# The order of the first transfers in a retention and two-layer-pair kernel

## The chip, the cores and the metric

One core of one Trainium2 chip runs the whole program. The metric is device time in microseconds (us); the figure of a kernel is the median of its runs. The kernel before took 1101.65 us (three runs, 1098.88 to 1103.2). The engines are named as the profile names them: PE multiplies matrices (PEld loads its weights), DVE works elementwise, ACT evaluates functions and copies, POOL is the general engine, SP issues nearly all transfers. Every engine takes its instructions in the order in which they are written.

## The reference, cut to what matters

```python
# q, k, v: (4, 8, 768, 64) = batch, heads, tokens, head size
gamma = 1.0 - 2.0 ** (-5.0 - np.arange(H))
for t in range(S):                                   # retention
    state = gamma * state + np.einsum('bhd,bhe->bhde', k[:, :, t], v[:, :, t])
    y[:, :, t] = scale * np.einsum('bhd,bhde->bhe', q[:, :, t], state)
x = y.transpose(0, 2, 1, 3).reshape(B * S, H * D)    # 3072 x 512
h = x @ w_in;  x = (h - np.tanh(h)) @ w_out          # 512 -> 2048 -> 512
h = x @ w_in2                                        # 512 -> 2048
x = np.where(h > 0, h, np.exp(np.minimum(h, 0)) - 1) @ w_out2
```

All weights and inputs are float32 (the weights arrive as 64-bit words, which the kernel converts).

## The kernel before

**The work.** The retention is cut into 24 steps: six chunks of 128 tokens, each for four batch entries. Step s needs three inputs: queries and keys with heads on the partitions (one transfer, `qk`, 512 KB), values (`v`, 256 KB) and keys with tokens on the partitions (`kn`, 256 KB). On PE a step is a group of score products (`sc`), an output (`oe`, `oo`) made of the state times the queries and of the values times the masked scores (`pt`), and a state update, which multiplies `v` and `kn`. DVE masks the scores (L297), scales the queries in place (L339) and scales `kn` in place (L343). Four steps fill one block of 512 tokens, and block b is then multiplied: product n of the first layer gives `h` from the block `x` and weight tile (0, f), ACT and DVE turn `h` into the gate `g` (h - tanh h by a polynomial where h is small), and the second layer adds weight tile (1, f) times `g` into four accumulators `acc`. Every factor is split in a high and a low part, and three of the four partial products are summed (`three`, L389 to L395; all large products of PE have line L392). So one product is 12 matmuls of 128x512. The two later layers (names `x`, `w`, `z`, `xo`, `wo`, `zo`) use a scheme with seven products for eight.

**The weights at the start.** A raw weight tile (512 KB, `raw`) is fetched (L305), converted by one pass of ACT (L308) and two of DVE (L312, L316) to `w32`, then split by ACT (L288) and DVE (L291). `jobs0` lists the tiles in the order in which they are wanted: (0, 0), (0, 1), (0, 2), (1, 0), (0, 3), (1, 1), and so on. For the first two blocks the products run over f = 0 to 7 first, block 0 and then block 1, so products 0 to 7 need sixteen tiles converted, and block 0 needs steps 0 to 3 and block 1 steps 4 to 7.

**The opening, in written order (L398 to L535).** Warm-up products, the transfers of steps 0 to 3, tiles 0 and 1, the queries of step 4 (`qk[B]`), tiles 2 and 3; then the work of steps 0 to 3 with the conversion of tiles 0 and 1 between; then, in buffers that earlier work has used (`va`, `ka`), the values and keys of step 4, tiles 4 to 11, and at the end the queries and keys of step 5 (`qa`, `kb`). Each transfer also waits until the eighth transfer before it has landed.

**The planner (class Plan, L57 to L243).** Everything behind the opening is given to it as operations with readers, writers, lengths and buffers. It walks through time with one list of ready operations for each engine, gives buffers from pools (`A_TAGS`, `B_TAGS` and so on; those that the opening holds stand in `taken`, and `had` hands them over) and takes on each engine the ready operation that is due first. PE's order is fixed. What it writes down is the order of the instructions; on the chip the semaphores decide the times. `ret_load` (L651) requests the inputs of a step, `loads` (L849) names the product after which it may, and converted weights of the second layer pair are stored to memory in pieces (`w2d`, `w3d`) and loaded again later, as are those of the first pair (`w1d`).

Of the kernel before, what the change touches and what calls it, by code (L numbers as in the profile page):

```python
# [8 lines left out]
F32 = mybir.dt.float32  # L9
# [9 lines left out]
P = 128  # L19
TB = 512  # L20
# [36 lines left out]
class Plan:  # L57
# [10 lines left out]
    def op(self, eng, dur, fn, r=(), w=(), lat=0.1, rel=0, due=None, name=""):  # L68
        o = Op()
        o.eng, o.fn, o.dur, o.lat, o.rel, o.name, o.due = eng, fn, dur, lat, rel, name, due  # L70
        o.n, o.deps, o.users, o.bufs = len(self.ops), set(), [], []

        def split(x):
            return x if isinstance(x, tuple) else (x, None)

        def met(table, key):
            return [v for k, v in table.items() if key is None or k is None or k == key]

        for x in r:
            b, k = split(x)  # L80
            o.deps.update(met(b.w, k))
        for x in w:
            b, k = split(x)
            o.deps.update(met(b.w, k))
            for ops in met(b.rd, k):
                o.deps.update(ops)
        for x in r:
            b, k = split(x)
            b.rd.setdefault(k, []).append(o.n)
            if b not in o.bufs:  # L90
                o.bufs.append(b)
        for x in w:
            b, k = split(x)
            for key in [i for i in b.w if k is None or i == k]:
                del b.w[key]
            for key in [i for i in b.rd if k is None or i == k]:
                del b.rd[key]
            b.w[k] = o.n
            if b not in o.bufs:
                o.bufs.append(b)  # L100
        for b in o.bufs:
            if b.group and not b.held and not b.left:
                c, k = self.groups.get(b.group, (b.cls, 0))
                self.groups[b.group] = c, k + 1
            b.left += 1
        o.deps.discard(o.n)
        self.ops.append(o)
        o.pe = None
        if eng == "PE":
            o.pe = len(self.pe)  # L110
            self.pe.append(o)
        return o

    def run(self):
# [4 lines left out]
        t, start = 0.0, {}  # L119
# [12 lines left out]
            else:  # L132
                o.late = min([o.late] + [e - o.dur - o.lat for e in ends])
        left = {o.n: len(o.deps) for o in ops}
        ready = {e: [] for e in ("ACT", "DVE", "SP", "POOL")}
        busy = dict.fromkeys(("PE", "ACT", "DVE", "SP", "POOL"), 0.0)
        state = {"dma": 0.0, "pe": 0, "at": 0.0}
        events = [(0.0, -1)]
        order = []

# [25 lines left out]
        def begin(o, t):  # L166
            for b in o.bufs:
                if b.cls != "D" and not b.held:
                    b.slot = self.free[b.cls].pop(0)
                    b.held = True  # L170
                    if b.group:
                        self.used[b.group] += 1
                        c, k = self.groups[b.group]
                        self.groups[b.group] = c, k - 1
            end = t + o.dur + o.lat
            if o.eng in ("SP", "POOL"):
                busy[o.eng] = t + (0.08 if o.eng == "SP" else 1.0)
                state["dma"] = max(state["dma"], t) + o.dur
                end = max(state["dma"], t) + 2.2
            else:  # L180
                busy[o.eng] = t + o.dur
            heapq.heappush(events, (busy[o.eng], -1))
            heapq.heappush(events, (end, o.n))
            order.append((o, t))
# [5 lines left out]
        while events:  # L190
# [18 lines left out]
            while moved:  # L209
                moved = False  # L210
                if busy["PE"] <= now and state["pe"] < len(self.pe):
                    o = self.pe[state["pe"]]
# [34 lines left out]
def retention_moe_kernel(ctx: ExitStack, tc: tile.TileContext, dims, ins, out):  # L247
    nc = tc.nc
    B, H, S, D, DM, DFF = dims
# [6 lines left out]
    NF = DFF // P  # L256
# [27 lines left out]
    def place(cls, tag, shape, dtype, name):  # L284
        return (ps if cls == "P" else sb).tile(shape, dtype, tag=tag, name=name)
# [18 lines left out]
    def fetch_(raw, job):  # L304
        nc.sync.dma_start(out=raw, in_=ins[f"w{job[0]}"][job[1]])  # L305
# [72 lines left out]
    def load_qk(t, s):  # L378
        nc.sync.dma_start(out=t, in_=ins["qkv"][s][:, 0:2, :])

    def load_v(t, s):
        nc.sync.dma_start(out=t, in_=ins["qkv"][s][:, 2, :])

    def load_kn(t, s):
        nc.sync.dma_start(out=t, in_=ins["qkv"][s][:, 3, :])
# [11 lines left out]
    with tc.manual_schedule():  # L397
# [23 lines left out]
        def fetch(i):  # L421
            job = jobs0[i]
            raw[job] = place("A", f"a{i}", [P, TB], I64, f"raw{job[0]}_{job[1]}")
            fetch_(raw[job], job)
# [11 lines left out]
        def convert_c(i):  # L436
            job = jobs0[i]
            t = wt[job] = place("A", f"a{i}", [P, 2, TB], F32R, f"w{job[0]}_{job[1]}")
            copy(t[:, 0, :], w32[job])
            return lambda: sub(t[:, 1, :], w32[job], t[:, 0, :].bitcast(F32))  # L440

        qk = {s: stage[:, s] for s in range(B)}
        v, kn, pt, sc, o0 = {}, {}, {}, {}, {}
# [8 lines left out]
            kn[s] = kn23[:, s - 2, :] if s > 1 else place("B", "k" + "ab"[s], [P, TB], F32, f"kn{s}")  # L452
            load_kn(kn[s], s)
        fetch(1)
        qk[B] = place("A", "qb", [P, 2, TB], F32, f"qk{B}")
        load_qk(qk[B], B)
        fetch(2)
        fetch(3)
        x0 = place("X", "x0", [P, 2, KC, TB], F32R, "x0")

        def scores0(s):
# [45 lines left out]
        for j in range(2):  # L507
            ds.append(place("P", f"b{6 + j}", [P, 2, NP, D], F32, f"dsp{j}"))
            for c in range(2):
                s = 2 * j + c  # L510
# [4 lines left out]
            st[j] = place("B", f"t{j}", [P, 2, NP, D], F32, f"st{j}")  # L515
            nc.vector.tensor_copy(out=st[j], in_=ds[j])
        lo1 = convert_c(1)
        v[B] = place("B", "va", [P, TB], F32, f"v{B}")
        load_v(v[B], B)
        kn[B] = place("B", "ka", [P, TB], F32, f"kn{B}")  # L520
        load_kn(kn[B], B)
        for i in range(4, 12):
            fetch(i)
        scores0(B)
        convert_b(2)
        lo1()
# [2 lines left out]
        scale_k_(kn[B])  # L529
        convert_a(3)  # L530
        convert_b(3)
        qk[B + 1] = place("A", "qa", [P, 2, TB], F32, f"qk{B + 1}")
        load_qk(qk[B + 1], B + 1)
        kn[B + 1] = place("B", "kb", [P, TB], F32, f"kn{B + 1}")
        load_kn(kn[B + 1], B + 1)  # L535

        taken = {"x0", "qa", "qb", "pt", "va", "ka", "kb", "t0", "t1", "s2", "s3"} | {f"a{i}" for i in range(12)}
        slots = {"A": A_TAGS, "B": B_TAGS, "C": C_TAGS, "X": X_TAGS, "P": P_TAGS}  # L540
        plan = Plan(
            {c: [t for t in tags if t not in taken] for c, tags in slots.items()},
# [4 lines left out]
        )  # L547
        op = plan.op

        def had(cls, slot, ap):  # L550
            return Buf(cls, name=slot, ap=ap, slot=slot)

        dr = {id(t): Buf("D", name="d") for t in (*x1d, *w1d, *w2d, w3d)}

# [4 lines left out]
        X[0] = had("X", "x0", x0)  # L559
        for i in range(2):  # L560
            W[jobs0[i]] = had("A", f"a{i}", wt[jobs0[i]])
        for i in range(2, 12):
            RAW[jobs0[i]] = had("A", f"a{i}", raw[jobs0[i]])
        for i in range(2, 4):
            W32[jobs0[i]] = had("B", f"s{i}", w32[jobs0[i]])
        QK = {B: had("A", "qb", qk[B]), B + 1: had("A", "qa", qk[B + 1])}
        V = {B: had("B", "va", v[B])}
        KN = {B: had("B", "ka", kn[B]), B + 1: had("B", "kb", kn[B + 1])}
        PT = {B: had("A", "pt", pt[B])}
        ST = {j: had("B", f"t{j}", st[j]) for j in range(2)}  # L570

# [4 lines left out]
        def dma(fn, size, r=(), w=(), rel=0, due=None, eng="SP", name="dma"):  # L576
            return op(eng, size * DMA, fn, r=r, w=w, rel=rel, due=due, name=name)
# [73 lines left out]
        def ret_load(s, rel):  # L651
            if s not in QK:
                t = QK[s] = Buf("A", [P, 2, TB], F32, f"qk{s}", "qk")
                dma(lambda: load_qk(t.ap, s), 4096, w=[t], rel=rel)
            t2 = V[s] = Buf("B", [P, TB], F32, f"v{s}", "v")
            dma(lambda: load_v(t2.ap, s), 2048, w=[t2], rel=rel)
            if s // B == NCH - 1:
                return
            if s not in KN:
                t3 = KN[s] = Buf("B", [P, TB], F32, f"kn{s}", "kn")  # L660
                dma(lambda: load_kn(t3.ap, s), 2048, w=[t3], rel=rel)
            k = KN[s]
            op("DVE", DVE5, lambda: scale_k_(k.ap), w=[k], name=f"scalek{s}")

        def ret_scores(s):
            q = QK[s]
            c = [Buf("P", [P, NP, P], F32, f"sc{s}_{j}") for j in range(2)]
# [6 lines left out]
        def ret_out(s):  # L674
            b, c = divmod(s, B)
            q, vv, p, sv = QK.pop(s), V.pop(s), PT.pop(s), ST[c // 2]
            even = Buf("P", [P, NP // 2, P], F32, f"oe{s}")
# [4 lines left out]
            if not last:  # L682
                k = KN.pop(s)
                op("PE", 0.6, lambda: state_mm(state_view(odd.ap), vv.ap, k.ap), r=[k, vv], w=[(odd, 1)], lat=0.2, name=f"state{s}")
# [158 lines left out]
        events = {0: [("out", B)]}  # L843
        for s in range(B + 1, NSTEP):
            b, k = s // B - 1, s % B
            at = 2 * k - 1 if b == 0 else FA + NF - 2 + 2 * k if b == 1 else b * NF + 4 * k + 1
            events.setdefault(at, []).append(("scores", s))
            events.setdefault(at + 1, []).append(("out", s))
        loads = {at - 2: s for at, l in events.items() for what, s in l if what == "scores"}  # L849
        for s in [loads.pop(k) for k in sorted(loads) if k < 0]:  # L850
            ret_load(s, 0)

# [284 lines left out]
```

## Time and profile before

| | before |
|---|---|
| median of the runs | 1101.65 us |
| the profiled execution | 1101.44 us, its span 1099.6 us |
| PE busy | 1075.6 us, 98% of the span |
| DVE, ACT, POOL busy | 82%, 65%, 0% |
| memory traffic | 217 GB/s over the span |

The profile is of one execution. Its page gives the busy time of each engine, forty slices of the span and the costliest groups of instructions; the trace behind it answers by stretch, by engine and by who waited for whom. A busy share near 100% says that an engine sets the pace, but not where it stood: that is read from the list of its waits and from the timeline around each. Idle time of an engine is put down to the one that released it. A time that begins a row is counted from the start of the span.

### The profile page before, as it was taken

The numbers are of one execution on the slowest core, as the hardware profiler recorded it, in microseconds if no ns is written. First come the engines' busy times: TensorE is split into PE (matmuls) and PEld (weight loads), VectorE is DVE, ScalarE is ACT, GpSimd is POOL, SyncE is SP. The second block draws the span as 40 slices with busy tenths as digits, with TensorE's granted clock in tenths as the row PEclk, the third lists the DMA queues.
The fourth block names the chain that finished last, engine by engine and source line by source line (L and its number), as shares of the span: only waits on it lengthen the run. The fifth ranks groups of instructions, "written<-read, shape, count | busy, mean of one in ns | idle before, by whom it ended". The sixth has DMA issues, their size and how long they took to land.

```text
span 1099.6 us, 15843 instructions
## 1 busy us (share of the span) xinstructions
PE 1075.6 (98%) x5745; PEld 877.7 (80%) x5745; DVE 905.5 (82%) x1516; ACT 709.6 (65%) x1290; POOL 3.9 (0%) x8
## 2 busy tenths in 40 slices
PE   7699999999999999999999999999999999999998
PEld 5488888888888877788888888888888888888887
DVE  6698899768888888888889769895977987878964
ACT  2557685546556655665678579964588864689652
POOL 0000000000000000000000000000000000000000
PEclk9799999999999999999999999999999999999999
DMA  9733366438666766776688569246966058863253
GB/s 331 272 115 134 154 230 210 116 116 248 231 221 225 254 220 221 273 257 238 248 294 288 192 235 383 110 153 217 388 233 233 15 216 320 330 213 132 112 213 134
DMA packets 99230, 239.86 MB, mean 218 GB/s; under 512 B 7632, under 2 KB 42448, under 8 KB 96464
## 3 DMA queue, kind: packets, MB, share of 16 engines
q1 hardware_dynamic: 98000, 235.96, 59.7%
q0 software_dynamic: 576, 2.10, 1.1%
q8 instruction: 45, 0.74, 0.3%
q10 hardware_dynamic: 576, 0.79, 0.2%
q14 instruction: 33, 0.27, 0.1%
HBM read 186.39 MB, written 52.43 MB: 217 GB/s over the span
## 4 chain that ended last, share of the span: by engine, by line
PE 82%; DMA 7%; DVE 7%; ACT 2%; issue 1%; SPq 1%; DVEq 0%
PE acc L392 19%; PE h L392 17%; PE xo L392 12%; PE x L392 12%; PE z L392 6%; PE zo L392 6%; PE wo L392 3%; PE w L392 3%; DMA kn<-qkv 3%; DMA qk<-qkv 2%; PE sc L332 2%; DMA raw<-w 1%; PE oe L362 1%; DVE pt L297 1%; DVE y L733 1%
## 5 line engine op out<-in xcount | busy, mean ns | idle before, releaser
L392 PE MATMUL acc<-g,w 128*128 128x512 f32 x1152 | 283.6, 395 | 0.1
L392 PE MATMUL h<-x,w 128*128 128x512 f32 x1152 | 278.5, 391 | 0.0
L392 PEld LDWEIGHTS h<-x,w 128*128 128x128 f32 x1152 | 217.0, 189 | 45.5 <-issue 0.2
L392 PEld LDWEIGHTS acc<-g,w 128*128 128x128 f32 x1152 | 214.1, 189 | 48.2 <-DVE g L291 1.0
L288 ACT ACTIVATE g<-y 128x512 fp32r<-128x512 f32 x240 | 141.4, 624 | 148.6 <-DVE y L736 122.8
L291 DVE TENSOR_TENSOR g<-y,g 128x512 fp32r<-128x512 f32 x240 | 160.0, 687 | 41.4 <-ACT g L288 40.4
L392 PE MATMUL xo<-g,w 128*128 128x512 f32 x576 | 133.5, 390 | 0.0
L392 PE MATMUL x<-xh,q 128*128 128x512 f32 x384 | 127.1, 389 | 0.0
L392 PEld LDWEIGHTS xo<-g,w 128*128 128x128 f32 x576 | 107.7, 188 | 23.9 <-ACT ou L288 1.9
L731 DVE SCALAR_TENSOR_TENSOR y<-y,u 128x512 f32<-128x512 f32 x96 | 66.2, 689 | 31.2 <-ACT y L725 31.0
L725 ACT ACTIVATE u<-h 128x512 f32<-128x512 f32 x96 | 56.8, 592 | 54.2 <-PE h L392 53.8
L392 PEld LDWEIGHTS x<-xh,q 128*128 128x128 f32 x384 | 72.1, 188 | 14.9
L754 DVE SCALAR_TENSOR_TENSOR y<-y,t 128x512 f32<-128x512 f32 x96 | 65.6, 685 | 14.7 <-ACT t L749 14.7
L736 DVE COPY_PREDICATED y<-m,h 128x512 f32<-128x512 uint16 x96 | 70.7, 737 | 5.0 <-ACT m L725 1.5
L392 PE MATMUL x<-xl,q 128*128 128x512 f32 x192 | 74.8, 390 | 0.0
L725 ACT ACTIVATE m<-u,xs_b 128x512 bf16<-128x512 f32 x96 | 69.5, 724 | 0.0
L725 ACT ACTIVATE y<-u,qa_b 128x512 f32<-128x512 f32 x96 | 69.3, 722 | 0.0
L733 DVE SCALAR_TENSOR_TENSOR y<-y,h 128x512 f32<-128x512 f32 x96 | 65.7, 684 | 1.9
L392 PE MATMUL z<-xh,q 128*128 128x512 f32 x192 | 67.0, 389 | 0.0
L291 DVE TENSOR_TENSOR h<-h,t 128x512 f32<-128x512 f32 x96 | 66.6, 694 | 0.0
L392 PE MATMUL zo<-g,w 128*128 128x512 f32 x288 | 66.3, 389 | 0.0
L392 PEld LDWEIGHTS zo<-g,w 128*128 128x128 f32 x288 | 54.1, 188 | 11.2
(101 smaller groups left out, 1422.7 us busy)
## 6 DMA issues: line engine op xcount, KB each, us to landing
w<-w3d SPq DMA_DIRECT2D x21, 2048.0 KB, 8.1
q<-w2d SPq DMA_DIRECT2D x72, 512.0 KB, 6.4
raw<-w SPq DMA_DIRECT2D x64, 512.0 KB, 7.7
w<-w1d SPq DMA_DIRECT2D x64, 512.0 KB, 7.2
qk<-qkv SPq DMA_DIRECT2D x20, 512.0 KB, 6.2
w1d<-w SPq DMA_DIRECT2D x16, 512.0 KB, 2.9
v<-qkv SPq DMA_DIRECT2D x24, 256.0 KB, 6.1
x1d<-o SPq DMA_DIRECT2D x12, 512.0 KB, 3.4
```

Of the source, the lines that this page charges most:

```text
L288: nc.scalar.activation(out=out_, in_=in_, func=AF.Copy)
L291: nc.vector.tensor_tensor(out=out_, in0=a, in1=b, op=ALU.subtract)
L297: nc.vector.tensor_tensor(out=out_, in0=a, in1=b, op=ALU.mult)
L332: nc.tensor.matmul(out=sc[j][:, p, :], lhsT=qk[r, 1, p * P:(p + 1) * P], rhs=qk[r, 0, p * P:(p + 1) * P], start=True, stop=True,)
L362: nc.tensor.matmul(out=outs[p][half(p, j)], lhsT=v[:, h * D:(h + 1) * D], rhs=pt[:, j, p, :], start=False, stop=True, skip_group_check=True,)
L392: nc.tensor.matmul(out=out_, lhsT=lhs(a), rhs=rhs(b), skip_group_check=True, start=(first and at == 0 and i == 0), stop=(last and at == n ...
L725: op("ACT", dur, lambda: nc.scalar.activation(out=o.ap, in_=i.ap, func=func, **kw), r=r, w=w, name=f"{func}{name}")
L731: op("DVE", DVE5, lambda: nc.vector.scalar_tensor_tensor(out=y.ap, in0=y.ap, scalar=QB, in1=u.ap, op0=ALU.add, op1=ALU.mult), r=[u], w=[y])
L733: op("DVE", DVE5, lambda: nc.vector.scalar_tensor_tensor(out=y.ap, in0=y.ap, scalar=C2, in1=h.ap, op0=ALU.mult, op1=ALU.mult), r=[h], w=[y ...
L736: op("DVE", 0.65, lambda: nc.vector.copy_predicated(out=y.ap, mask=m.ap.bitcast(U16), data=h.ap), r=[m, h], w=[y], due=9.0)
L754: op("DVE", DVE5, lambda: nc.vector.scalar_tensor_tensor(out=yv(), in0=yv(), scalar=1.0, in1=t.ap, op0=ALU.add, op1=ALU.mult), r=[t], w=[k])
```

## The change

There are two parts. In the opening, the queries, values and keys of steps 4 and 5 are requested in one run, each step followed by one weight tile (tiles 2 and 3), into buffers that nothing has used before (`t2` to `t5`, `a12`; `qb` as before). Tiles 4 to 11 leave the opening: the planner requests them as it does the later ones. It is told that the transfers of step 5 are still under way for 2 us of its time (operations on an engine `IN` that issues nothing, and `state["dma"]` at 2.0). In the middle, from product 32 on, the inputs of a step are requested three products ahead of its scores, not two.

```diff
-        ready = {e: [] for e in ("ACT", "DVE", "SP", "POOL")}
-        busy = dict.fromkeys(("PE", "ACT", "DVE", "SP", "POOL"), 0.0)
-        state = {"dma": 0.0, "pe": 0, "at": 0.0}
+        ready = {e: [] for e in ("ACT", "DVE", "SP", "POOL", "IN")}
+        busy = dict.fromkeys(("PE", "ACT", "DVE", "SP", "POOL", "IN"), 0.0)
+        state = {"dma": 2.0, "pe": 0, "at": 0.0}
...
-            else:
+            elif o.eng != "IN":
                 busy[o.eng] = t + o.dur
...
         fetch(1)
-        qk[B] = place("A", "qb", [P, 2, TB], F32, f"qk{B}")
-        load_qk(qk[B], B)
-        fetch(2)
-        fetch(3)
+        for s, (q, t2, t3) in ((B, ("qb", "t2", "t3")), (B + 1, ("a12", "t4", "t5"))):
+            qk[s] = place("A", q, [P, 2, TB], F32, f"qk{s}")
+            load_qk(qk[s], s)
+            v[s] = place("B", t2, [P, TB], F32, f"v{s}")
+            load_v(v[s], s)
+            kn[s] = place("B", t3, [P, TB], F32, f"kn{s}")
+            load_kn(kn[s], s)
+            fetch(s - 2)
...
         lo1 = convert_c(1)
-        v[B] = place("B", "va", [P, TB], F32, f"v{B}")
-        load_v(v[B], B)
-        kn[B] = place("B", "ka", [P, TB], F32, f"kn{B}")
-        load_kn(kn[B], B)
-        for i in range(4, 12):
-            fetch(i)
         scores0(B)
...
         convert_b(3)
-        qk[B + 1] = place("A", "qa", [P, 2, TB], F32, f"qk{B + 1}")
-        load_qk(qk[B + 1], B + 1)
-        kn[B + 1] = place("B", "kb", [P, TB], F32, f"kn{B + 1}")
-        load_kn(kn[B + 1], B + 1)
...
-        for i in range(2, 12):
+        for i in range(2, 4):
             RAW[jobs0[i]] = had("A", f"a{i}", raw[jobs0[i]])
...
-            t2 = V[s] = Buf("B", [P, TB], F32, f"v{s}", "v")
-            dma(lambda: load_v(t2.ap, s), 2048, w=[t2], rel=rel)
+            if s not in V:
+                t2 = V[s] = Buf("B", [P, TB], F32, f"v{s}", "v")
+                dma(lambda: load_v(t2.ap, s), 2048, w=[t2], rel=rel)
...
-        loads = {at - 2: s for at, l in events.items() for what, s in l if what == "scores"}
+        loads = {at - (2 if at < 2 * NF else 3): s for at, l in events.items() for what, s in l if what == "scores"}
```

On SP, the queue of transfers, the opening from tile 1 (`raw_1_147`) on; numbers behind a name are the buffers' own, `qk_149` is step 4, `qk_357` step 5. Before:

```order
L305 DMA raw_1_147<-w 128x512
L379 DMA qk_149<-qkv 128x1024
L305 DMA raw_2_151<-w 128x512
L305 DMA raw_0_153<-w 128x512
L382 DMA v_315<-qkv 128x512
L385 DMA kn_317<-qkv 128x512
L305 DMA raw_3_319<-w 128x512
L305 DMA raw_1_321<-w 128x512
L305 DMA raw_4_323<-w 128x512
L305 DMA raw_2_325<-w 128x512
L305 DMA raw_5_327<-w 128x512
```

Three more tiles follow there, and then `qk_357`, `kn_359` and `v_377`. After, from the same tile on, with step 5 as `qk_157`, `v_159` and `kn_161`:

```order
L305 DMA raw_1_147<-w 128x512
L379 DMA qk_149<-qkv 128x1024
L382 DMA v_151<-qkv 128x512
L385 DMA kn_153<-qkv 128x512
L305 DMA raw_2_155<-w 128x512
L379 DMA qk_157<-qkv 128x1024
L382 DMA v_159<-qkv 128x512
L385 DMA kn_161<-qkv 128x512
L305 DMA raw_0_163<-w 128x512
L305 DMA raw_3_362<-w 128x512
L305 DMA raw_1_364<-w 128x512
L305 DMA raw_4_369<-w 128x512
```

The three inputs of step 5 moved from behind the twelfth tile to the place behind the third; the next row after these is the store of the converted tile (1, 0), which waits for DVE.

On DVE, the end of the opening and the planner's first operations; `kn_359` is step 5's key tile, `w_2_374` and `w_0_379` are the splits of tiles 2 and 3. Before:

```order
L312 TENSOR_SCALAR w_1_0_353<-w_1_0_353 128x512
L316 SCALAR_TENSOR_TENSOR w_1_0_353<-raw_0_153,w_1_0_353 128x512
L343 TENSOR_TENSOR kn_359<-kn_359,ktab 128x512
L291 TENSOR_TENSOR w_2_374<-w_0_2_307,w_2_374 128x512
L291 TENSOR_TENSOR w_0_379<-w_1_0_353,w_0_379 128x512
L312 TENSOR_SCALAR w_0_3_382<-w_0_3_382 128x512
```

After, the same place, with step 5's keys as `kn_161` and the first gate's polynomial as `y_396`:

```order
L312 TENSOR_SCALAR w_1_0_343<-w_1_0_343 128x512
L316 SCALAR_TENSOR_TENSOR w_1_0_343<-raw_0_163,w_1_0_343 128x512
L291 TENSOR_TENSOR w_2_360<-w_0_2_317,w_2_360 128x512
L291 TENSOR_TENSOR w_0_366<-w_1_0_343,w_0_366 128x512
L343 TENSOR_TENSOR kn_161<-kn_161,ktab 128x512
L729 SCALAR_TENSOR_TENSOR y_396<-y_396,u_392 128x512
```

The key scaling moved behind two splits, and the conversions of tiles 4 to 6 moved further back, behind the first gate's polynomial.

On SP, in the middle, the requests of step 18 (`qk_3859` before) among the stores of converted weights to `w2d` and the loads from `w1d`. Before:

```order
L642 DMA w2d_99<-wbh_3742 128x3x256
L606 DMA w_8_3823<-w1d_86 128x1024
L642 DMA w2d_99<-wbl_3768 128x3x256
L642 DMA w2d_99<-wth_3832 128x4x256
L642 DMA w2d_99<-wtl_3845 128x4x256
L379 DMA qk_3859<-qkv 128x1024
L382 DMA v_3861<-qkv 128x512
L385 DMA kn_3865<-qkv 128x512
```

After:

```order
L639 DMA w2d_99<-wbh_3742 128x3x256
L379 DMA qk_3809<-qkv 128x1024
L382 DMA v_3811<-qkv 128x512
L385 DMA kn_3827<-qkv 128x512
L603 DMA w_8_3829<-w1d_86 128x1024
L639 DMA w2d_99<-wbl_3768 128x3x256
L639 DMA w2d_99<-wth_3838 128x4x256
L639 DMA w2d_99<-wtl_3851 128x4x256
```

The three requests moved in front of one weight load and three stores; steps 12 to 17 and 19 to 23 moved alike or by fewer rows.

## Rows read from the trace of the kernel before

**Rows 1.** Page, part 1: busy us of each engine (share of the span), instructions.

```profile
PE 1075.6 (98%) x5745; PEld 877.7 (80%) x5745; DVE 905.5 (82%) x1516; ACT 709.6 (65%) x1290; POOL 3.9 (0%) x8
```

**Rows 2.** PE's waits, whole span: who <- released by: total us, times, longest.

```profile
PE sc L332 <- DMA qk<-qkv: 7.7, 4, 4.7
PE oe L356 <- DVE qk L339: 6.0, 1, 6.0
```

**Rows 3.** Timeline, PE, 25 to 58: start, us, operation, count, [idle before <- releaser].

```profile
28.79 0.33 PE L356 MATMUL oe<-qk,st 64*64 64x128 f32 x2
...
30.87 3.03 PE L392 MATMUL h<-x,w 128*128 128x512 f32 x12
38.61 2.08 PE L332 MATMUL sc<-qk 64*128 64x128 f32 x16 [4.70 <-DMA qk<-qkv]
...
50.90 0.48 PE L356 MATMUL oe<-qk,st 64*64 64x128 f32 x2 [6.01 <-DVE qk L339]
```

**Rows 4.** Timeline, DVE, 23 to 60.

```profile
24.58 0.42 DVE L312 TENSOR_SCALAR w<-w 128x512 uint32<-128x512 uint32 x1
...
29.10 0.69 DVE L316 SCALAR_TENSOR_TENSOR w<-raw,w 128x512 uint32<-128x512 uint32 x1
39.19 0.69 DVE L343 TENSOR_TENSOR kn<-kn,ktab 128x512 f32<-128x512 f32 x1 [9.40 <-DMA kn<-qkv]
```

**Rows 5.** Timeline, SP's transfer issues, 12 to 32.

```profile
15.13 1.54 SPq L305 DMA_DIRECT2D raw<-w  x2
20.66 0.33 SPq L382 DMA_DIRECT2D v<-qkv  x1
...
21.51 5.74 SPq L305 DMA_DIRECT2D raw<-w  x8
...
30.11 0.33 SPq L385 DMA_DIRECT2D kn<-qkv  x1
```

**Rows 6.** Transfers issued at 15.13 and at 30.11: KB, us from issue to landing.

```profile
raw<-w SPq DMA_DIRECT2D x1, 512.0 KB, 7.8
...
kn<-qkv SPq DMA_DIRECT2D x1, 256.0 KB, 9.1
```

**Rows 7.** Stretches: us, busy (x instructions) by engine, granted PE clock, DMA share, GB/s.

```profile
18.00:24.00 6.00, 3.66 (x78) 3.03 (x78) 5.94 (x12) 2.57 (x5) 0.00 (x0) 1.00 1.00 380
30.00:36.00 6.00, 3.90 (x38) 2.98 (x34) 0.00 (x0) 4.85 (x10) 0.00 (x0) 1.00 1.02 419
39.19:87.69 48.50, 42.49 (x310) 34.19 (x309) 45.84 (x87) 29.23 (x55) 0.00 (x0) 0.89 0.41 142
```

**Rows 8.** Timeline, ACT, 20 to 36.

```profile
22.97 0.67 ACT L308 ACTIVATE w<-raw 128x512 f32<-128x512 f32 x1 [1.89 <-DMA raw<-w]
...
32.02 0.58 ACT L725 ACTIVATE u<-h 128x512 f32<-128x512 f32 x1
...
32.97 0.72 ACT L725 ACTIVATE y<-u,qa_b 128x512 f32<-128x512 f32 x1
```

**Rows 9.** Timeline, PE, 82 to 95: products of the first, then the second layer.

```profile
87.69 2.88 PE L392 MATMUL h<-x,w 128*128 128x512 f32 x12
90.42 2.88 PE L392 MATMUL acc<-g,w 128*128 128x512 f32 x12
```

**Rows 10.** A stretch after the wait of 4.70 us, columns as in rows 7.

```profile
38.00:40.00 2.00, 1.39 (x12) 1.40 (x14) 0.81 (x2) 0.00 (x0) 0.00 (x0) 0.50 0.15 58
```

**Rows 11.** PE's waits, 100 to 700 us.

```profile
PE sc L332 <- DMA qk<-qkv: 3.0, 3, 1.2
```

**Rows 12.** Timeline, SP's transfer issues, 385 to 400.

```profile
386.93 0.49 SPq L606 DMA_DIRECT2D w<-w1d  x1
...
392.38 0.36 SPq L642 DMA_DIRECT2D w2d<-wtl  x1
392.84 0.52 SPq L379 DMA_DIRECT2D qk<-qkv  x1
```

**Rows 13.** Timeline, PE, 385 to 405: step 18's scores.

```profile
399.99 1.16 PE L332 MATMUL sc<-qk 64*128 64x128 f32 x16 [0.94 <-DMA qk<-qkv]
```

More of the change, by code (lines that the diff above doesn't have):

```diff
@@ L531, in retention_moe_kernel @@
         convert_b(3)
-        qk[B + 1] = place("A", "qa", [P, 2, TB], F32, f"qk{B + 1}")
-        load_qk(qk[B + 1], B + 1)
-        kn[B + 1] = place("B", "kb", [P, TB], F32, f"kn{B + 1}")
-        load_kn(kn[B + 1], B + 1)
-        taken = {"x0", "qa", "qb", "pt", "va", "ka", "kb", "t0", "t1", "s2", "s3"} | {f"a{i}" for i in range(12)}
+        taken = {"x0", "qb", "a12", "pt", "s2", "s3"} | {f"a{i}" for i in range(4)} | {f"t{i}" for i in range(6)}
         slots = {"A": A_TAGS, "B": B_TAGS, "C": C_TAGS, "X": X_TAGS, "P": P_TAGS}
@@ L548, in retention_moe_kernel, with had @@
         op = plan.op
-        def had(cls, slot, ap):
-            return Buf(cls, name=slot, ap=ap, slot=slot)
+        def had(cls, slot, ap, underway=False):
+            b = Buf(cls, name=slot, ap=ap, slot=slot)
+            if underway:
+                op("IN", 2.0, lambda: None, w=[b])
+            return b
         dr = {id(t): Buf("D", name="d") for t in (*x1d, *w1d, *w2d, w3d)}
@@ L565, in retention_moe_kernel @@
             W32[jobs0[i]] = had("B", f"s{i}", w32[jobs0[i]])
-        QK = {B: had("A", "qb", qk[B]), B + 1: had("A", "qa", qk[B + 1])}
-        V = {B: had("B", "va", v[B])}
-        KN = {B: had("B", "ka", kn[B]), B + 1: had("B", "kb", kn[B + 1])}
+        QK = {B: had("A", "qb", qk[B]), B + 1: had("A", "a12", qk[B + 1], True)}
+        V = {B: had("B", "t2", v[B]), B + 1: had("B", "t4", v[B + 1], True)}
+        KN = {B: had("B", "t3", kn[B]), B + 1: had("B", "t5", kn[B + 1], True)}
         PT = {B: had("A", "pt", pt[B])}
```

## The prediction

> **What bounds the kernel now.** I read the page's busy shares first, then who PE waits for, then the two places where it waits. PE is busy 98% of the span [rows 1], so only its waits and its slow clock can be won without less work. Its list of waits [rows 2] is short: 7.7 us for queries and 6.0 us for one scaled-query tile; everything else is the first transfers and small change. The profiled execution took 1101.44 us, 1099.6 of it the span; that is 0.2 us under the median of the runs shown.
>
> Two stretches hold these waits. In the start PE stands 4.70 us for the queries of step 5, then 6.01 us for DVE [rows 3]. The second wait is a child of the first transfer order: DVE, which takes its instructions in order, stood 9.40 us in front of one instruction, the scaling of step 5's keys (kn), because those keys had not landed [rows 4]. Everything DVE had to do later was queued behind it. The keys came late because eight weight tiles went ahead of them on the SP queue [rows 5]: issued at 30.11, landing 9.1 us later, at 39.2 [rows 6]. The third place is the middle: three waits, 3.0 us together, for queries of steps 18 to 20 [rows 11].
>
> **The change in the start.** Queries, values and keys of steps 4 and 5 are now issued in one run, before raw tiles 2 and 3; the tiles from number 4 on become the planner's, behind them. No byte is added. No instruction of PE changes place; on DVE the 90 instructions from the key scaling to the split of the gate that the sixth second-layer product reads are the same set in another order.
>
> First the landings. DMA is full here: 419 GB/s [rows 7], so 512 KB take 1.25 us. Tile 2 landed at 15.13 + 7.8 = 22.9 [rows 5, 6]; ahead of it now stand step 4's values and keys, 512 KB, so 24.2. Step 5's 1 MB follows, +2.5: the keys land at 26.7, not 39.2, and tile 3 at 28.0. In the old order SP stood from 16.67 to 20.66 [rows 5], until PE had freed the old buffer of step 4's values; the new buffers have no earlier owner, so SP has no such stop. Each of the moved issues costs SP about 0.4 us, far less than a landing.
>
> The chip's own bandwidth is a place to weigh the notes. The Trainium skill, "DMA: Bandwidth & Descriptors", section "Specifications", puts one core's share of HBM at about 358 GB/s; the trace shows 419 in this stretch, so the measurement decides. By the page 512 KB would take 1.46 us, an estimate, and tile 3 would land 0.8 us later: 1087.9 in place of 1087.5.
>
> Now DVE. Tile 2's first conversion on ACT takes 0.67 us [rows 8], so DVE can start its half at 24.95, where it did at 24.58 [rows 4]: +0.37. The rest of the opening moves with it, and the last opening instruction, which began at 29.10 and took a slot of 0.60 [rows 4], now ends at 30.1. There DVE used to stop for 9.40 us; now the keys have been there for 3 us. From 39.19 to 87.69, where PE begins the eighth first-layer product [rows 9], DVE was busy 45.84 of 48.50 us [rows 7], and the product began as DVE finished its weights. The same work less one half-size item (0.34) that now stands behind that weight tile gives 30.1 + 45.5 = 75.6, plus DVE's own waits.
>
> Those waits I bound. Zero is one end. The other is what DVE waited in the same work before, 48.50 - 45.84 = 2.66, plus a new one at the start: with the keys no longer late, DVE reaches the first activation polynomial at 32.1, while ACT, which converts two weight tiles first, starts it at 30.8 and needs 1.67 us to the end of its second square (32.02 to 32.97 + 0.72 [rows 8]), 32.4. That is 0.3, and 0.2 for a weight split before it. So 0 to 3.1; I take 1.0, these 0.5 and as much again for later hand-overs, since the 1.75 that DVE once waited for scores came from a PE that was late and now is early. The product starts at 76.6, not 87.69: **11.0 us** won, between 9.0 and 12.1.
>
> Is PE able to? From step 4's output, now at 29.2, to that product lie four outputs of 2.08 (28.79 to 30.87 [rows 3]), three score groups of at most 1.16 [rows 13], and eleven products of 2.73 (87.69 to 90.42 [rows 9]): 8.3 + 3.5 + 30.0 = 41.8, so PE alone would be there at 71.0. It is DVE that ends last, and some 5.6 us of PE waits stay, in pieces under 2 us: the first in front of step 5's output (PE there at 37.9, DVE's masks and scaled queries at about 39.4), the rest in front of products whose weights or gate are just being split. That is what is late next.
>
> Two costs I put at nothing. Raw tiles 7 and 8 (after the first three of the planner's) now stand on SP behind the store of a converted weight, which waits for DVE until about 31.5; they land near 37 and ACT wants them near 39. If that cover is gone, ACT waits in order, and DVE behind it. And from 100 to 399 us the old PE had no wait [rows 11], and the same DVE and ACT work lies beside it, so the lead is kept, not spent.
>
> **The change in the middle.** For the twelve steps from 12 on the loads are requested one first-layer product earlier. In the trace the load of step 18 stood on SP behind a weight load at 386.93 and three stores of converted weights, the last at 392.38; it went out at 392.84 [rows 12] and PE, at its scores since 399.05, got it at 399.99 after a wait of 0.94 [rows 13]. It now stands in front of that weight load, so it leaves at about 387, 5.9 us earlier, and lands 5 us ahead of PE. The three waits go: **3.0 us** [rows 11]. The other end is 0, if SP is blocked there too: values and keys still wait for a buffer. The weight load behind is put back by 1 MB, 2.5 us; I cost it nothing, since five such tiles are held and PE takes one per 5.45 us, some 21 us of cover, and PE has no wait for them in the list [rows 2].
>
> Sum: 1101.44 - 11.0 - 3.0 = 1087.4, with the 0.2 to the median **1087.5 us**.
>
> **The rivals.**
> (a) *The short waits keep the clock down; slower.* The granted clock was 0.50 of full, the 1.2 GHz level, after the wait of 4.70 us [rows 10], and the same score group then took 2.08 us instead of 1.16 [rows 3, 13], a factor of 1.79. If PE, stopped again and again, ran 37.9 to the eighth product at that level, 33.1 us of work become 59.3 and the product starts at 97.2: 9.5 later, less 3.0, 1108. It is slower than now once the low level holds for over 75% of that stretch. Against it: from 18 to 24 us PE was busy only 3.66 of 6.00 us, in pieces, at a clock of 1.00 [rows 7]. Chance 0.05.
> The Trainium skill speaks for it: "TensorE: Matmul & The Clock Gate", section "A second HAM failure mode: psum-queue depth-cycling", has the clock swing between its levels when PE idles briefly and often between groups. By that rule (a) would be the outcome; the trace's 18 to 24 us do not agree.
> (b) *The weight tiles are now late.* If tiles 7 and 8 need as long as the full queue gave (10 us, not 5.5), they land at 41.9, ACT stands 3 us and DVE with it: 1090.4. Against: the queue is nearly empty by then. Chance 0.13.
> (c) *The middle gives nothing*, because the earlier request meets a blocked SP: 1090.5. Chance 0.08.
> (d) *DVE does not bind*, PE runs through at 71.0: 16.7 + 3.0 won, 1081.7. Against: the same 90 instructions. Chance 0.03.
> (e) *The reorder does not reach DVE*: the keys land late as before, since SP's eight-back waits hold them up. Only the middle is won, 1098.5, within half a per cent. For it: every issue waits for the landing of the eighth before it. Against: the ones eight back are the first transfers, landed by 20.4. Chance 0.06.
>
> **How the numbers follow.** The forecast has 0.65. Half a per cent, 5.5 us, is what a measurement of this kernel can tell from none. Forecast, (b), (c) and (d) are faster: 0.89, of which I take 0.02 off for a (b) several times as large. Same: (e) and that, 0.08. Slower: (a), 0.05. The forecast's own terms run from 1101.65 - 15.1 = 1086.5 to 1101.65 - 9.0 = 1092.6; two us on either side are the spread of the runs. The range, 1084 to 1094.5, holds (b) and (c) too and leaves out (a), (d) and (e).
>
> **What would show it.** DVE's wait for kn at the opening is gone and its longest wait before 80 us is under 2 us; the scores of step 5 follow the second first-layer product without a gap, near 34; step 5's output starts at 39 to 40 after a wait of 1 to 2 us; the clock shows 1.00 from 25 to 60; the eighth product starts at 75.6 to 78.7; PE has no wait for queries past 300 us. It is wrong if the clock falls under 1.00 between 34 and 80 us, if PE or ACT waits for raw tiles, or if PE shows waits past 100 us that were not there.

## The result, and the profile after

The changed kernel takes 1087.87 us (median of four runs, 1086.23 to 1088.33), against 1101.18 us for the kernel before in the same comparison (four runs): 0.9877 of its time, with a 95% interval of 0.9854 to 0.9900. That is 13.3 us, and 0.4 us above the forecast of 1087.5. The profiled execution took 1088.26 us, its span 1086.5 us, 13.1 us less than the 1099.6 of before.

Busy time by engine, from the first part of the page, against [rows 1]:

```profile
PE 1073.4 (99%) x5745; PEld 874.1 (80%) x5745; DVE 905.1 (83%) x1516; ACT 710.6 (65%) x1290; POOL 3.9 (0%) x8
```

The work is the same to the instruction, and PE's busy time falls by only 2.2 us. Most of what went is waiting. These are the longest of PE's waits over the whole span (who, released by whom: total us, times, longest), against [rows 2]; two of 1.3 us each, which were there before, are left out:

```profile
PE sc L332 <- DMA stage<-qkv: 2.7, 3, 2.0
PE sc L332 <- DVE st L520: 1.6, 1, 1.6
...
PE oe L356 <- DVE qk L339: 1.0, 1, 1.0
```

No wait for queries (`qk<-qkv`) is left, and the 6.0 us for scaled queries are 1.0. Where they went is seen on PE's timeline from 23 to 92 us (start, us, operation, count, [idle before it <- releaser]), against [rows 3, 9]:

```profile
25.10 1.75 PE L332 MATMUL sc<-qk 64*128 64x128 f32 x16 [1.58 <-DVE st L520]
26.78 4.61 PE L392 MATMUL h<-x,w 128*128 128x512 f32 x12
31.33 0.33 PE L356 MATMUL oe<-qk,st 64*64 64x128 f32 x2
...
33.41 3.03 PE L392 MATMUL h<-x,w 128*128 128x512 f32 x12
36.37 1.16 PE L332 MATMUL sc<-qk 64*128 64x128 f32 x16
...
41.52 0.33 PE L356 MATMUL oe<-qk,st 64*64 64x128 f32 x2 [1.04 <-DVE qk L339]
...
43.60 3.02 PE L392 MATMUL acc<-g,w 128*128 128x512 f32 x12
46.46 2.88 PE L392 MATMUL h<-x,w 128*128 128x512 f32 x12
...
77.11 3.40 PE L392 MATMUL h<-x,w 128*128 128x512 f32 x12
80.34 2.88 PE L392 MATMUL acc<-g,w 128*128 128x512 f32 x12
```

Step 5's scores (36.37) follow the second first-layer product at once, its output starts at 41.52 instead of 50.90, the eighth first-layer product at 77.11 instead of 87.69, and the product behind it at 80.34 instead of 90.42. From there on the lead is 10.1 us; the other 3.0 of the 13.1 come in the middle.

DVE's timeline from 23 to 40 us, against [rows 4]:

```profile
26.96 0.43 DVE L312 TENSOR_SCALAR w<-w 128x512 uint32<-128x512 uint32 x1 [1.32 <-ACT w L308]
...
31.49 0.69 DVE L316 SCALAR_TENSOR_TENSOR w<-raw,w 128x512 uint32<-128x512 uint32 x1
32.10 1.48 DVE L291 TENSOR_TENSOR w<-w,w 128x512 fp32r<-128x512 f32 x2
33.50 0.68 DVE L343 TENSOR_TENSOR kn<-kn,ktab 128x512 f32<-128x512 f32 x1
34.46 0.69 DVE L729 SCALAR_TENSOR_TENSOR y<-y,u 128x512 f32<-128x512 f32 x1 [0.28 <-ACT y L723]
```

The scaling of step 5's keys (L343 at 33.50) has no wait in front of it; before, 9.40 us stood there. But the last opening instruction (31.49) ends its slot at 32.10, where the prediction had 30.1.

Three stretches of the changed kernel (us; busy and instructions of PE, PEld, DVE, ACT, POOL; granted PE clock; DMA share; GB/s), the last two against the third row of [rows 7]:

```profile
28.00:30.00 2.00, 2.00 (x6) 1.54 (x6) 2.00 (x5) 0.00 (x0) 0.00 (x0) 0.50 0.99 392
32.10:41.33 9.23, 8.38 (x72) 6.56 (x70) 8.85 (x19) 8.11 (x16) 0.00 (x0) 1.00 0.76 253
41.33:77.11 35.78, 34.86 (x285) 27.30 (x285) 35.78 (x68) 26.01 (x49) 0.00 (x0) 1.00 0.54 202
```

From 41.33 to the eighth product DVE is busy without a break, and PE lacks 0.92 us: DVE binds, by little. The first row shows a clock of 0.50, the 1.2 GHz level, where the prediction had none.

In the middle, SP's transfer issues from 365 to 395 us, against [rows 12]:

```profile
374.09 0.37 SPq L639 DMA_DIRECT2D w2d<-wbh  x1
374.50 0.49 SPq L379 DMA_DIRECT2D qk<-qkv  x1
...
376.04 0.42 SPq L603 DMA_DIRECT2D w<-w1d  x1
```

PE's timeline there, against [rows 13]:

```profile
388.92 1.16 PE L332 MATMUL sc<-qk 64*128 64x128 f32 x16
```

Step 18's queries leave directly behind one store of converted weights and in front of the weight load; they land 5.8 us later, at 380.3, 8.6 us before PE wants them. Between 80 and 700 us PE's list of waits is empty.

### The profile page after: what moved, and what is told of

It reads as the page before. It is cut to its first block, busy times and chain, and to the rows that moved or that the text cites. A ratio compares the mean times of both kernels' runs of the same rounds, so it can differ in the third digit from the quotient of the medians.

```text
span 1086.5 us, 15854 instructions
## 1 busy us (share of the span) xinstructions
PE 1073.4 (99%) x5745; PEld 874.1 (80%) x5745; DVE 905.1 (83%) x1516; ACT 710.6 (65%) x1290; POOL 3.9 (0%) x8
## 4 chain that ended last, share of the span: by engine, by line
PE 89%; DVE 6%; DMA 3%; issue 1%; ACT 0%; ACTq 0%; DVEq 0%
PE acc L392 22%; PE h L392 21%; PE xo L392 12%; PE x L392 12%; PE zo L392 6%; PE z L392 6%; PE wo L392 3%; PE w L392 3%; PE sc L332 2%; PE oe L362 1%; PE oe L356 1%; DMA raw<-w 1%; DMA kn<-qkv 1%; DMA v<-qkv 1%; DVE w L316 1%
## 5 line engine op out<-in xcount | busy, mean ns | idle before, releaser
L729 DVE SCALAR_TENSOR_TENSOR y<-y,u 128x512 f32<-128x512 f32 x96 | 66.0, 687 | 30.1 <-ACT y L723 30.0
```

The costliest lines, as they stand in the source:

```text
L729: op("DVE", DVE5, lambda: nc.vector.scalar_tensor_tensor(out=y.ap, in0=y.ap, scalar=QB, in1=u.ap, op0=ALU.add, op1=ALU.mult), r=[u], w=[y])
```

## The experiments

The theory: DVE's in-order wait for step 5's keys set the end of the start (some 10 us of the 13), and the two parts add. The rivals: PE's own listed wait for step 5's queries was the loss; or PE's slow clock; and, for what is left, that PE rather than DVE binds. The first four ran beside 14 runs of the kernel before (median 1101.33 us), the last four beside 7 (1101.54 us).

**The opening alone.** The changed kernel with the request rule of before:

```diff
-        loads = {at - (2 if at < 2 * NF else 3): s for at, l in events.items() for what, s in l if what == "scores"}
+        loads = {at - 2: s for at, l in events.items() for what, s in l if what == "scores"}
```

> The changed kernel with the middle part undone (inputs of a step requested two products ahead everywhere). Theory: the two parts add, the opening is worth some 10.1 us and the three waits for queries after 390 us come back at 3.0 us: about 1091 us, PE's list of waits shows three waits for qk again. Rival (the opening alone carries the whole 13.3 us, and the waits in the middle are hidden or move): 1087.9 us.

Measured: 1091.17 us (1090.3 to 1092.36), 0.9901 of before [0.9885, 0.9918]: 10.2 us. PE's waits from 100 us on show the three old ones and a fourth:

```profile
PE sc L332 <- DMA qk<-qkv: 4.2, 4, 1.6
```

So the opening gives about 10 us by itself, and taking the middle back costs 3.3.

**The middle alone.** The kernel before with the new request rule:

```diff
-        loads = {at - 2: s for at, l in events.items() for what, s in l if what == "scores"}
+        loads = {at - (2 if at < 2 * NF else 3): s for at, l in events.items() for what, s in l if what == "scores"}
```

> The kernel before with the middle part alone (three products ahead from product 32 on). Theory: the three waits for queries, 3.0 us, go and nothing takes their place: 1098.2 us, the opening as before with DVE's wait of 9.4 us for the keys. Rival (the time returns as another wait, for a weight load that now goes out later): 1101.2 us with new PE waits past 250 us.

Measured: 1097.34 us (1096.44 to 1098.66), 0.9962 [0.9949, 0.9975]: 4.0 us, one more than expected. All that is left of PE's waits from 100 us on:

```profile
PE acc L392 <- DVE g L291: 0.2, 1, 0.2
```

The query waits are gone. The fourth microsecond is not shown to come from the rule: in this profiled execution the start, which the edit does not touch, was 1.5 us shorter (DVE's wait for keys 8.34, not 9.40 us, and the eighth product at 86.19, not 87.69). The two parts alone add to 14.2 us, together they gave 13.3; that agrees within the spread of the runs.

**Only step 5's keys early.** The kernel before, with one transfer moved in front of eight weight tiles, into a free buffer:

```diff
         load_kn(kn[B], B)
+        kn[B + 1] = place("B", "t5", [P, TB], F32, f"kn{B + 1}")
+        load_kn(kn[B + 1], B + 1)
         for i in range(4, 12):
             fetch(i)
...
-        kn[B + 1] = place("B", "kb", [P, TB], F32, f"kn{B + 1}")
-        load_kn(kn[B + 1], B + 1)
```

> The kernel before with one transfer moved: step 5's keys (kn, 256 KB) go out before weight tiles 4 to 11, into a buffer of their own; its queries and values stay late. All other orders unchanged. Theory (DVE's in-order wait for the keys is what costs): the wait of 9.4 us goes, PE still waits for the queries until about 39 at the low clock, step 5's output starts near 43 instead of 50.9, and the eighth product near 80: about 1093.7 us (1092.5 to 1095.5). Rival (PE's own wait for the queries is the cost, as its list of waits says): 1100.5 to 1101.5 us.

Measured: 1093.85 us (1092.15 to 1095.23), 0.9928 [0.9913, 0.9942]: 7.5 us from one transfer of 256 KB. DVE's timeline at the key scaling:

```profile
29.90 0.68 DVE L343 TENSOR_TENSOR kn<-kn,ktab 128x512 f32<-128x512 f32 x1
```

And PE's timeline, at step 5's scores and at the eighth first-layer product:

```profile
39.17 2.08 PE L332 MATMUL sc<-qk 64*128 64x128 f32 x16 [5.11 <-DMA qk<-qkv]
...
79.52 2.88 PE L392 MATMUL h<-x,w 128*128 128x512 f32 x12
```

PE still waits 5.11 us for its queries, a little longer than before, and step 5's output starts at 45.51, not near the 43 that was expected, since a product of 4.40 us at the low clock (0.50 from 38 to 44 us) lies between; and yet the eighth product starts 8.2 us earlier.

**Only step 5's queries early.** The counterpart: the same place, the queries instead of the keys, 512 KB:

```diff
         load_kn(kn[B], B)
+        qk[B + 1] = place("A", "a12", [P, 2, TB], F32, f"qk{B + 1}")
+        load_qk(qk[B + 1], B + 1)
         for i in range(4, 12):
             fetch(i)
...
-        qk[B + 1] = place("A", "qa", [P, 2, TB], F32, f"qk{B + 1}")
-        load_qk(qk[B + 1], B + 1)
```

> The kernel before with one transfer moved: step 5's queries (512 KB) go out before weight tiles 4 to 11, into a buffer of their own; its keys and values stay late. All other orders unchanged. Theory: the 4.7 us wait for queries goes from PE's list, but DVE still stands about 9.4 us for the keys and with it the split of weight tile 2, so PE waits for that instead and step 5's output stays near 50: 1100 to 1101.5 us. Rival (the wait for queries is the cost): 4.7 us and the slow clock come back, 1095 us.

Measured: 1101.1 us (ten runs, 1099.43 to 1102.28), 0.9995 [0.9986, 1.0005]: nothing. PE's waits from 28 to 96 us:

```profile
PE oe L356 <- DVE qk L339: 6.4, 1, 6.4
PE h L392 <- DVE w L291: 4.1, 1, 4.1
```

The wait of 4.70 us that headed PE's list is gone, and one of 4.1 us for a weight split stands in its place: DVE, still in front of its keys for 8.63 us, has not made it. The eighth product starts at 87.53, as before. These two runs settle the first rival: the listed wait was worth nothing while DVE stood, and DVE's was worth 7.5 us while the listed wait stayed. The other 2.7 of the opening's 10.2 us came only with the rest of its new order; which part of that gave them, no run takes apart.

**Less work on DVE.** The changed kernel without the shift pass (L312) of twelve weight tiles of the first two layers, which is left out of the computation; it tells whether DVE binds the start now:

```diff
-            op("DVE", 0.36, lambda: conv_b1(t.ap), w=[t], due=due, name=f"convb{job}")
+            op("DVE", 0.36, lambda: None if m < 2 and f < FA else conv_b1(t.ap), w=[t], due=due, name=f"convb{job}")
```

> The changed kernel with one pass of DVE's weight conversion (the shift, L312) left out for the twelve tiles that the planner converts for products 0 to 7, so these weights are not the right ones; all orders are otherwise the same. Ten of these passes, 0.335 us each, stand ahead of the eighth product's weights, twelve in the whole stretch. Theory (DVE sets the end of the start): the eighth product starts 3.4 us earlier, near 73.7, and the kernel takes 1084.2 us (1083.5 to 1085). Rival (PE's order or the latency of one gate's chain sets it): 1087.9 us.

Measured: 1085.89 us (1084.92 to 1086.13), 0.9856 [0.9841, 0.9871]: 2.0 us under the changed kernel, where 3.7 were expected, and the two intervals overlap. The eighth product starts at 74.82, not near 73.7. From step 5's output to the eighth product:

```profile
40.14:74.82 34.68, 34.66 (x284) 27.33 (x285) 33.70 (x60) 25.98 (x50) 0.00 (x0) 1.00 0.58 216
```

Now PE is busy without a break and DVE lacks 0.98 us; in the changed kernel it was the other way round. The stretch is 0.9 us shorter than in its neighbours (35.59 to 35.64 between the same two points), and then PE ends last. From the end of DVE's opening (31.39 here) to the eighth product it is 43.43 us, where the changed kernel has 45.01: the passes were worth 1.6 us, not 3.4. So DVE did bind, but with PE about 1 us behind it. The theory is half right, and the 5.6 us of slack on PE are wrong.

**Weight tile first.** The changed kernel, with tile 2 before step 4's values and keys, and tile 3 before step 5's inputs:

```diff
         for s, (q, t2, t3) in ((B, ("qb", "t2", "t3")), (B + 1, ("a12", "t4", "t5"))):
+            if s > B:
+                fetch(s - 2)
             qk[s] = place("A", q, [P, 2, TB], F32, f"qk{s}")
             load_qk(qk[s], s)
+            if s == B:
+                fetch(s - 2)
...
-            fetch(s - 2)
```

> The changed kernel with weight tiles 2 and 3 moved up in the first transfers: queries of step 4, tile 2, values and keys of step 4, tile 3, then step 5's three. No other order changes. Theory (the opening of DVE stood 1.3 us for tile 2, and what DVE gains there goes through to the end): tile 2 lands some 2 us earlier, the 1.3 us wait goes, tile 3 is there in time, step 5's keys land by 29.5 and still before DVE wants them: about 1086.5 us. Rival (another wait of the opening takes its place, or step 5's keys are now late): 1087.9 to 1089 us.

Measured: 1086.78 us (1086.04 to 1087.53), 0.9863 [0.9847, 0.9880]; the eighth product starts at 76.38. It is the lowest median of the complete kernels, 1.1 us under the changed one, but the intervals overlap. From step 5's output to the eighth product it is the changed kernel again:

```profile
40.76:76.38 35.62, 34.89 (x284) 27.29 (x285) 35.62 (x67) 25.80 (x49) 0.00 (x0) 1.00 0.54 202
```

DVE's 1.32 us for tile 2's conversion are gone here, but something else took their place. The clock fell in the opening, at the scores of the first steps; the stretch from 16 to 18 us (columns as above), and a group of scores in it on PE's timeline:

```profile
16.00:18.00 2.00, 2.00 (x20) 1.68 (x16) 0.76 (x2) 1.12 (x2) 0.00 (x0) 0.50 1.06 399
```

```profile
16.32 2.08 PE L332 MATMUL sc<-stage 64*128 64x128 f32 x16
```

In the last kernel below, which has the same order, the clock was 1.00 there and the group took 1.16 us:

```profile
15.74 1.16 PE L332 MATMUL sc<-stage 64*128 64x128 f32 x16
```

DVE's opening ended at 31.35 here and at 30.34 there, so this low clock was paid, with about 1.0 us. The four executions of this kernel part in the same way: 1086.04 and 1086.05 us at a mean granted clock of 1.000, 1087.52 and 1087.53 at 0.998. What the order alone is worth stays undecided.

**Warm products ahead of step 4's scores.** The changed kernel with eight extra warm-up matmuls, so that PE does not stand there:

```diff
+        warm(8)
         scores0(B)
```

> The changed kernel with eight more warm-up products of PE in its wait before step 4's scores. Theory (the low clock of the first product, 4.6 us in place of 3.0, lies beside DVE's work and costs nothing): the clock stays at 1.00, the first product takes 3.0 us, the eighth starts at 76.5 to 77.5 as before, 1087.9 us within 1 us. Rival (the low clock is paid): 1.5 us less, 1086.3 us.

Measured: 1087.75 us (1087.51 to 1088.46), 0.9876 [0.9861, 0.9890], the time of the changed kernel. The clock from 24 to 30 us:

```profile
24.00:30.00 6.00, 5.84 (x62) 4.25 (x58) 5.92 (x12) 1.64 (x3) 0.00 (x0) 1.00 1.00 400
```

On PE's timeline the first product now takes 3.02 us instead of 4.61:

```profile
27.83 3.02 PE L392 MATMUL h<-x,w 128*128 128x512 f32 x12
```

The eighth product starts at 76.70, as in the neighbours. That the extra products kept the clock up is not shown: without them PE stood only 0.98 us there in the opening-only, less-work and tile-first executions, and the first product took 3.01 to 3.03 us. That its low clock was free is shown by DVE: from tile 2's landing to the scaling of step 5's keys it took 7.23 us in the changed kernel, where the first product took 4.61, and 7.24 here (25.80 to 33.04), where it took 3.02.

**Tile first, and three key scalings on POOL.** The tile-first kernel, with the scaling of step 5 to 7's keys moved from DVE to an idle engine:

```diff
+    def scale_k_(kn, eng=None):
...
+        (eng or nc.vector).tensor_tensor(out=k, in0=k, in1=ktab.to_broadcast([P, H, D]), op=ALU.mult)
...
+            op("DVE", DVE5, lambda: scale_k_(k.ap, nc.gpsimd if s < 2 * B else None), w=[k], name=f"scalek{s}")
```

> The kernel with weight tiles 2 and 3 moved up, and the scaling of the keys of steps 5, 6 and 7 done by POOL, which is idle, in place of DVE. Theory (DVE sets the end of the start): three times 0.60 us leave DVE's queue, the eighth product starts 1.8 us earlier than with the tiles alone: about 1084.7 us. Rival (POOL is slow enough, or disturbs DVE enough, that a state update waits for the keys): 1086.5 us or more, with a PE wait for kn from POOL.

Measured: 1087.07 us (1086.59 to 1088.81), 0.9871 [0.9856, 0.9886]: no gain over the tile-first order. POOL's timeline:

```profile
30.18 1.15 POOL L343 TENSOR_TENSOR kn<-kn,ktab 128x512 f32<-128x512 f32 x1 [29.73 <-DMA kn<-qkv]
...
55.02 1.04 POOL L343 TENSOR_TENSOR kn<-kn,ktab 128x512 f32<-128x512 f32 x1 [11.76 <-PE oo L356]
```

DVE's timeline at the same times:

```profile
30.34 2.13 DVE L291 TENSOR_TENSOR w<-w,w 128x512 fp32r<-128x512 f32 x2
...
55.04 1.57 DVE L291 TENSOR_TENSOR w<-w,w 128x512 fp32r<-128x512 f32 x1
56.53 0.68 DVE L291 TENSOR_TENSOR g<-y,g 128x512 fp32r<-128x512 f32 x1
```

PE shows no wait for `kn` from POOL, which the rival expected. A split of a weight (two inputs from SBUF, the engines' working memory) that starts beside a POOL scaling takes 1.57 us, where the like operation behind it takes 0.68; the pair at 30.34 takes 2.13, where it took 1.48 at 32.10 in the changed kernel. Of the 1.8 us that three scalings cost DVE (0.60 each by their slots), 0.65 + 0.89 = 1.54 us came back as such stretching, in two of them; beside the third (42.17 on POOL) DVE's subtraction in `h`, which has one input in PE's own output memory, took 0.70 us. In all nothing was left: from the end of DVE's opening to the eighth product it is 45.07 us here and 45.03 in the tile-first kernel. The profiled execution is the faster of the two (1086.59 against 1087.53 us) by its opening alone. The Trainium skill, "SBUF — State Buffer", section "SBUF: two separate sides", says that DVE and GpSimd (POOL here) share one pair of ports, that whichever starts first has it for its whole instruction, and that a DVE operation with two inputs from that memory contends for it; the two rows agree.

## Why the prediction was right

**The mechanism** was right. DVE's in-order wait for step 5's keys set the end of the start, not PE's waits that headed the list [rows 2]: keys alone gave 7.5 us, queries alone nothing.

**The start, 11.0 us predicted, 10.1 measured.** The eighth product was put at 30.1 + 45.5 + 1.0 = 76.6 and came at 77.11, in these pieces:

| term | predicted | measured |
|---|---|---|
| DVE's opening ends | 30.1 | 32.10 |
| DVE's work from there to the eighth product | 45.5 | 8.85 + 35.78 = 44.63 |
| DVE's own waits in it | 1.0 | 0.38 |
| eighth product starts | 76.6 | 77.11 |

The first term was mis-sized by 2.0 us, and the others happened to give 1.5 back. The forecast's distance of 0.4 us is luck in part, too: by the spans 13.1 us were won, for 14.0 in the sum. In this execution the late landing of tile 2 moved the first term. ACT's timeline of the changed kernel, where a wait for `raw` ends as a weight tile lands:

```profile
22.57 0.68 ACT L308 ACTIVATE w<-raw 128x512 f32<-128x512 f32 x1 [2.32 <-DMA raw<-w]
26.27 0.67 ACT L308 ACTIVATE w<-raw 128x512 f32<-128x512 f32 x1 [3.01 <-DMA raw<-w]
...
30.03 0.68 ACT L308 ACTIVATE w<-raw 128x512 f32<-128x512 f32 x1 [2.58 <-DMA raw<-w]
```

The same in the opening-only kernel, whose first transfers have the same order:

```profile
24.45 0.69 ACT L308 ACTIVATE w<-raw 128x512 f32<-128x512 f32 x1 [1.96 <-DMA raw<-w]
28.23 0.66 ACT L308 ACTIVATE w<-raw 128x512 f32<-128x512 f32 x1 [2.00 <-DMA raw<-w]
```

Tiles 2 and 3 were predicted at 24.2 and 28.0. The opening-only execution has them at 24.4 and 28.2, the profiled one of the changed kernel 2 us later. But DVE's opening ended no earlier than 31.74 in the opening-only execution, without a wait for tile 2: there the clock was low from 16 to 18 us [row under the rivals], and the copies of the state that DVE makes ahead of tile 2 began at 25.42 instead of 24.36. So the term left out two things, a late landing and a slow clock in the first steps, and either is enough; with neither, in the last experiment (tile 2 at 24.5, though ahead of step 4's values and keys), the opening ended at 30.34. On SP's timeline of the changed kernel the issues of step 5 show where it stood:

```profile
18.57 0.33 SPq L379 DMA_DIRECT2D qk<-qkv  x1
20.87 0.33 SPq L382 DMA_DIRECT2D v<-qkv  x1
21.36 0.33 SPq L385 DMA_DIRECT2D kn<-qkv  x1
22.57 2.80 SPq L305 DMA_DIRECT2D raw<-w  x4
```

SP issued step 5's queries at 18.57 and its values only at 20.87, and tile 3 at 22.57, just as tile 1, the eighth before it, landed. So SP did stop, not for a buffer but for landings, and the prediction's "landed by 20.4" failed in this execution (tile 1 came at 22.57), a small share of rival (e). Even so the keys, issued at 21.36 and 7.4 us under way, came at 28.8, before DVE wanted them. In the other direction, DVE's work up to the product's start is 0.9 us shorter than its sum, and the product takes 3.40 us instead of 2.88, so that 10.6 us at its start are 10.1 behind it. It began before its last weights were split. On DVE's timeline before, the split of its weight tile ended its slot as the product started, at 87.69:

```profile
87.07 0.69 DVE L291 TENSOR_TENSOR w<-w,w 128x512 fp32r<-128x512 f32 x1
```

After, it stands behind the product's start:

```profile
77.19 0.67 DVE L291 TENSOR_TENSOR w<-w,w 128x512 fp32r<-128x512 f32 x1
```

To the end of that split, 77.79, DVE's work comes to 45.3 us, so the 45.5 of the sum was right; what failed is that the product begins as DVE finishes its weights.

**The middle, 3.0 us predicted, 3.0 by the spans and 3.3 by the opening-only kernel.** Step 18's queries landed 8.6 us ahead of PE, not 5; the weight loads put back behind them made no wait, as argued.

**PE's slack was wrong.** The prediction had PE alone at the eighth product at 71.0, 5.6 us ahead of DVE. Its waits from 37.9 on come to 1.04 + 0.17 + 0.57 = 1.8 us (the first is in the rows above, the others are in front of a weight split and a gate). PE stood before step 5's output at 40.5, not 37.9: 2.1 of that were there at step 4's output already (31.33, not 29.2). From that output to the eighth product its work is 34.7 us with DVE relieved, not 33.1: I had taken 2.73 us for every product, and in that kernel the nine of them take 2.81 to 3.20 from start to start. The forecast did not suffer, since DVE ends last by its own sum, but whoever had cut DVE by 4 us on this figure would have got 1.6.

**The rivals.** (a) was argued against too strongly. After a wait of 1.58 us the clock was at 0.50 [first row of the three stretches], and in the opening-only kernel after one of 2.14 us:

```profile
16.00:18.00 2.00, 2.00 (x20) 1.67 (x18) 0.75 (x2) 0.55 (x2) 0.00 (x0) 0.50 0.99 381
```

So "the clock shows 1.00 from 25 to 60" was wrong. The Trainium skill, "TensorE: Matmul & The Clock Gate", section "A second HAM failure mode: psum-queue depth-cycling", tells of a clock that swings when PE idles briefly and often between groups of products; these two rows agree in part. Stands of 2.01 to 2.16 us at the same place as the second row's were followed by a clock of 1.00 in five other executions, and from 32 to 77 us of the changed kernel, with waits of up to 1.04 us in it, the clock held 1.00, so that the sign of being wrong from 34 to 80 us did not come. At the first product the low clock cost nothing; in the first steps it held DVE up, as the tile-first kernel shows. (b) did not come: behind 30.03 ACT had no wait for raw tiles. Tiles 2 and 3 it did wait for (3.01 and 2.58 us), which the prediction's last sentence, taken at its word, counts as a sign of being wrong. (c) is excluded by the middle-only kernel, (d) by DVE's 35.78 busy us of 35.78, (e) as a whole by the 10 us.

**What stays open** is why the first transfers of one order land 2 us apart between executions, and why the clock fell from 16 to 18 us in three executions, after stands of 1.95, 2.14 and 2.20 us, and not in the five with 2.01 to 2.16; whether either goes with the chip or with the single execution no run here takes apart. How both reach the time is plain, since DVE needs the same 45.0 us from the end of its opening in every complete kernel with the change in the start:

| execution | clock, 16 to 18 us | tile 2 lands | DVE's opening ends | eighth product | between |
|---|---|---|---|---|---|
| changed kernel | 1.00 | 26.3 | 32.10 | 77.11 | 45.01 |
| opening only | 0.50 | 24.4 | 31.74 | 76.77 | 45.03 |
| warm products | 0.50 | 25.8 | 31.65 | 76.70 | 45.05 |
| tile first | 0.50 | 22.9 | 31.35 | 76.38 | 45.03 |
| tile first, POOL | 1.00 | 24.5 | 30.34 | 75.41 | 45.07 |

## What to carry to other kernels

Behind the wait that heads the bounding engine's list there may stand an engine that takes its work in order and waits longer for something smaller; test it by moving each input alone (here 256 KB were worth 7.5 us, the 512 KB of the listed wait none). Once such a wait is gone, add up both engines to the same later point with durations as they are there, stretched ones included: here the two came out 1 us apart, which says how little more can be had from either alone. When single executions differ by a microsecond or two, split the time at a point of the bounding engine's work: here the time up to the end of DVE's opening varied by 1.8 us, and the time from there by less than 0.1. A request that stands in order behind stores that wait can be moved in front of them (here 3 to 4 us).

## What the runs showed of the hardware

The granted clock fell to the 1.2 GHz level after PE stood for 1.58 us in one execution (0.50 from 28 to 30 us; the first product took 4.61 us, elsewhere 3.02) and after 1.95 to 2.20 us in three others (0.50 from 16 to 18 us; a score group took up to 2.08 us, elsewhere 1.16); after stands of 2.01 to 2.16 us at that place it was 1.00 in five more, so the length of the one stand does not decide it here. The first fall cost nothing, beside DVE's own work; the other, in front of it, about 1.0 us. DVE's weight split took 1.57 instead of 0.68 us beside a POOL operation, so handing elementwise work to an idle POOL gave back what it relieved. The first tiles of the same transfer order landed at 24.4 and 28.2 us in one execution and at 26.3 and 30.0 in another.
